# Delta-rule attention with two MLPs: weights converted and split during the attention, half of the second MLP's kept on chip, fillers in another bank, and a searched order

## The chip, the core and the metric

The kernel runs on one core of a Trainium2 chip. Its time is device microseconds (us) of one execution. TensorE (PE) multiplies into PSUM; VectorE (DVE), ScalarE (ACT) and GpSimd (POOL) do the rest; SyncE's queue (SP) issues nearly all transfers between the on-chip memory and DRAM.

## What is computed

Three stages follow one another. `_attn_ref` goes through 768 positions of 32 heads one by one; `_moe_ref` and `_moe2_ref` are two-layer MLPs on 3072 tokens of width 384, with 2048 hidden units and two different activations.

```
for t in range(S):
    kt, vt, bt = (k_n[:, :, t], v[:, :, t], beta[:, :, t, None])
    y[:, :, t] = np.einsum('bhd,bhde->bhe', q[:, :, t], state)
    v_old = np.einsum('bhde,bhd->bhe', state, kt)
    state = state + bt[:, :, :, None] * np.einsum('bhd,bhe->bhde', kt, vt - v_old)
...
P = a[0] + a[1] * h + a[2] * h2 + a[3] * h3
Q = 1.0 + np.abs(b[0]) * np.abs(h) + np.abs(b[1]) * h2
g = P / (Q + 1e-06)
...
sp = np.where(h > 20.0, h, np.log1p(np.exp(np.minimum(h, 20.0))))
g = h * np.tanh(sp)
```

The four weight matrices arrive as 64-bit floats. The kernel turns them into 32-bit ones with integer operations on their two words, and splits every 32-bit operand of an MLP into a high part and the remainder, so that three matmuls replace one.

## The kernel before

**Attention** (line numbers are those of the profile). The 768 positions are 12 chunks of 64, called u. `prepare` (L264) loads and normalizes k and q of a chunk, transposes them (L317) and forms their products (L332), which DVE masks into `gm` and `lg` (L341). `inverse` (L384) takes two chunks together: DVE transposes `lg` (L402), then DVE or POOL runs 30 dependent pairs of small operations (L414, L420) between two scalings by beta (L405, L424), and DVE transposes the result into `xt` (L427). `ON_DVE = (1, 7)` puts the inverses of chunks 0, 1 and 6, 7 on DVE, the other four on POOL. There is one `lg`. `step` (L444) is the recurrence: each chunk needs the state `su` of the one before and its own `xt`: PE (L474, L491, L506, L514, L529), DVE (L482) and ACT (L498, L522, L538) in turn, for two halves of the heads.

**Order.** `Plan` collects these operations with an estimated duration, what they read and write, and a due time (`early`), and lists them by the longest path that remains (`order`, L90). Every engine then runs its part in that order. Where the plan leaves PE idle, `run` (L128) puts in fillers: matmuls of a zero tile (`heat`, L1010) into 128 columns of the PSUM tile `side`. The other 384 columns of `side` hold the DVE's intermediate words of the weight conversion.

**Weights.** `Weights.convert` (L609) handles one of the two matrices of one f (f counts 16 slices of 128 hidden units): a load into `w64` (L616), `mag` on ACT (L628), four DVE operations (L633, L637, L643, L649) into `wm`. During the attention all 32 matrices of the first MLP are converted; those of f = 0 are split into their slot (L659 on ACT, L664 on POOL), the other 30 go unsplit to DRAM (L657). `fetch`, `hi` and `lo` (L684 to L695) bring an f back, copy its high part on ACT (L689) and subtract on POOL or DVE (L693).

**MLPs.** A unit is one group of 512 tokens (six groups) with one f, so 96 units an MLP. A unit has nine matmuls up (L784), elementwise work, and four units later its matmuls down: nine of 512 columns (L870) in the first MLP, twelve of 384 (L903) in the second. `MLP_OPS` lists, for four kinds of unit, in which order the operations of a unit and of older ones are issued; kinds 0, 2 and 3 contain the split `wa`, `wb`, `wB`. The first MLP splits f = 1 to 15 in its first 15 units, from two `wraw` buffers. The second's matrices are converted by `Conv`: 16 of 32 spread over the first MLP, the rest in the first units of the second, four thirds of a matrix a unit; each goes to DRAM, comes back and is split.

## Time and profile before

| | us |
|---|---|
| median of 3 runs (1221.35 to 1222.2) | 1221.74 |
| the profiled execution | 1227.12 |
| its span, from the first to the last instruction | 1225.4 |
| attention, to the start of the first MLP's first matmul | 341.1 |
| first MLP, its first 17 units up | 97.0 |
| first MLP, from there to the second's first matmul | 337.9 |
| second MLP, first 16 units | 101.6 |
| second MLP, the rest | 347.8 |

The stages were cut where PE's matmuls change lines (L784 begins at 341.1, L903's unit 96 at 775.97); the first MLP's units begin one after another, so 341.1 and 438.1 are the starts of units 0 and 17, and 877.56 that of unit 112. The profiled execution is 5.4 us over the median. Engines are busy for 1074.0 us (PE), 756.6 (DVE), 604.9 (ACT) and 520.8 (POOL) of the span, which says little, since the stages differ: PE works without gaps in the last, and in the others something else decides.

### The profile page before, as it was taken

How to read it: one execution, taken by the hardware profiler on the slowest of the kernel's cores; microseconds unless marked ns; L12 is line 12 of the kernel's file. 1: busy time of each engine (PE TensorE's matmuls, PEld its weight loads, DVE VectorE, ACT ScalarE, POOL GpSimd, SP SyncE). 2: the span in 40 equal slices, each digit the busy share in tenths (PEclk: the TensorE clock that was granted, in tenths of full speed). 3: DMA queues.
4: the chain of work that ended last, by engine and by line, in shares of the span. 5: the costliest groups of instructions: out<-in, count | busy, mean ns of one | idle time of the engine just before them, and what ended most of it. 6: DMA issues, size and time to landing. Idle time of an engine off the chain costs nothing.

```text
span 1225.4 us, 24811 instructions
## 1 busy us (share of the span) xinstructions
PE 1074.0 (88%) x10210; PEld 924.5 (75%) x10210; DVE 756.6 (62%) x1226; ACT 604.9 (49%) x1063; POOL 520.8 (42%) x582
## 2 busy tenths in 40 slices
PE   6658876687759899999999999967899999999998
PEld 5557765687746578777787778766799999999997
DVE  5876689775448989989898999876412121212111
ACT  4325533342246788788888888732332333232222
POOL 3184757446036667667676777863300000000000
PEclk9959899697669999999999999988899999999999
DMA  6326743365332310212111121255200000000000
GB/s 119 80 60 155 171 120 87 93 171 137 111 91 68 106 59 28 69 46 65 46 48 63 40 72 28 91 191 167 84 27 26 26 27 26 26 26 1 21 7 26
DMA packets 128322, 89.01 MB, mean 73 GB/s; under 512 B 80592, under 2 KB 113232, under 8 KB 128208
## 3 DMA queue, kind: packets, MB, share of 16 engines
q1 hardware_dynamic: 127952, 87.32, 26.3%
q8 instruction: 80, 1.31, 0.5%
q14 instruction: 34, 0.28, 0.1%
q0 software_dynamic: 256, 0.10, 0.1%
HBM read 61.05 MB, written 26.35 MB: 71 GB/s over the span
## 4 chain that ended last, share of the span: by engine, by line
PE 41%; POOL 13%; DVE 12%; ACT 10%; issue 7%; DMA 5%; SPq 0%; POOLq 0%; DVEq 0%; ACTq 0%
PE h L784 17%; PE o L903 14%; POOL q L827 7%; ACT r L834 3%; POOL r L817 3%; POOL gh L799 2%; ACT q L814 2%; PE c_ps L491 2%; DMA w<-in_moe_w_in_dram 2%; ACT r L836 2%; PE y_ps L529 2%; PE o L870 2%; DMA w<-in_moe_w_out_dram 1%; DVE wm L649 1%; PE c_ps L506 1%
## 5 line engine op out<-in xcount | busy, mean ns | idle before, releaser
L784 PE MATMUL h<-x,w 128*128 128x512 f32 x1728 | 448.3, 404 | 54.9 <-ACT g L894 22.9
L784 PEld LDWEIGHTS h<-x,w 128*128 128x128 f32 x1728 | 327.4, 193 | 139.3 <-ACT g L894 25.2
L799 DVE TENSOR_TENSOR gh<-g,gh 128x512 fp32r<-128x512 f32 x82 | 57.0, 695 | 278.4 <-ACT g L894 278.4
L903 PE MATMUL o<-w,gh 128*128 128x384 f32 x1152 | 218.6, 338 | 0.0
L870 PE MATMUL o<-gh,w 128*128 128x512 f32 x864 | 214.2, 392 | 0.4 <-ACT ev L992 0.4
L903 PEld LDWEIGHTS o<-w,gh 128*128 128x128 f32 x1152 | 206.8, 190 | 8.4
L870 PEld LDWEIGHTS o<-gh,w 128*128 128x128 f32 x864 | 163.2, 189 | 36.5 <-ACT ev L992 2.1
L889 ACT ACTIVATE gh<-h 128x512 fp32r<-128x512 f32 x96 | 57.5, 599 | 218.0 <-PE h L784 217.9
L827 POOL TENSOR_TENSOR q<-q,r 128x512 f32<-128x512 f32 x96 | 127.2, 1325 | 64.7 <-ACT r L821 59.6
L799 POOL TENSOR_TENSOR gh<-g,gh 128x512 fp32r<-128x512 f32 x110 | 150.8, 1371 | 3.0 <-ACT gh L795 3.0
L817 POOL TENSOR_SCALAR r<-q,ab 128x512 f32<-128x512 f32 x61 | 48.8, 800 | 113.3 <-ACT q L814 113.3
L834 ACT ACTIVATE r<-q,cst 128x512 f32<-128x512 f32 x96 | 66.4, 691 | 55.3 <-POOL q L827 55.3
L850 DVE SCALAR_TENSOR_TENSOR q<-q,r 128x512 f32<-128x512 f32 x96 | 65.6, 683 | 25.6 <-ACT r L836 25.4
L841 DVE TENSOR_TENSOR s<-s,h 128x512 f32<-128x512 f32 x96 | 65.4, 681 | 17.1 <-ACT s L823 17.0
L823 ACT ACTIVATE s<-h,ab 128x512 f32<-128x512 f32 x96 | 74.2, 773 | 0.0
L843 DVE SCALAR_TENSOR_TENSOR s<-s,ab,h 128x512 f32<-128x512 f32 x96 | 71.8, 748 | 3.4
L491 PE MATMUL c_ps<-r,xt 32*32 32x48 f32 x1536 | 48.8, 225 | 26.9 <-DVE r L482 22.0
L814 ACT ACTIVATE q<-h 128x512 f32<-128x512 f32 x96 | 57.3, 597 | 30.3 <-PE h L784 26.2
L854 DVE SCALAR_TENSOR_TENSOR r<-s,ab,r 128x512 f32<-128x512 f32 x96 | 71.9, 749 | 0.0
L1012 PE MATMUL side<-ident,zero 128*128 128x128 f32 x194 | 32.4, 323 | 41.0 <-DVE wm L649 17.1
L859 DVE SCALAR_TENSOR_TENSOR g<-q,r 128x512 f32<-128x512 f32 x96 | 65.9, 687 | 3.3
L491 PEld LDWEIGHTS c_ps<-r,xt 32*32 32x32 f32 x1536 | 43.0, 123 | 31.9 <-DVE r L482 22.7
(116 smaller groups left out, 1403.9 us busy)
## 6 DMA issues: line engine op xcount, KB each, us to landing
w<-in_moe_w_in_dram SPq DMA_DIRECT2D x32, 384.0 KB, 3.7
w<-in_moe_w_out_dram SPq DMA_DIRECT2D x32, 384.0 KB, 3.6
w<-wm SPq DMA_DIRECT2D x62, 192.0 KB, 3.6
wraw<-w SPq DMA_DIRECT2D x31, 384.0 KB, 3.1
xraw<-x SPq DMA_DIRECT2D x36, 256.0 KB, 2.8
kn<-in_k_dram SPq DMA_DIRECT2D x48, 96.0 KB, 3.5
qn<-in_q_dram SPq DMA_DIRECT2D x48, 96.0 KB, 3.6
v<-in_v_dram SPq DMA_DIRECT2D x48, 96.0 KB, 3.4
```

Source lines behind the costliest of these rows:

```text
L491: nc.tensor.matmul(out=out(h, rows, n), lhsT=xt[rows, u % 2 * M + W * h + n, :], rhs=r2[rows, W * h + n, :], start=True, stop=True,)
L784: self.nc.tensor.matmul(out=self.st[i]["h"], lhsT=self.w.t[f][:, a, 0, k], rhs=self.x[g][:, b, k], start=(n == 0), stop=(n == 8),)
L799: (nc.gpsimd if engine == "P" else nc.vector).tensor_tensor(out=s["gh"][:, 1], in0=s["g"], in1=s["gh"][:, 0].bitcast(F32), op=ALU.subtract)
L814: nc.scalar.activation(out=s["q"], in_=s["h"], func=ACTF.Abs)
L817: nc.gpsimd.tensor_scalar(out=s["r"], in0=s["q"], scalar1=k["b1"], scalar2=k["b0"], op0=ALU.mult, op1=ALU.add)
L823: nc.scalar.activation(out=s["s"], in_=s["h"], func=ACTF.Identity, scale=k["a3"], bias=k["a2"])
L827: nc.gpsimd.tensor_tensor(out=s["q"], in0=s["q"], in1=s["r"], op=ALU.mult)
L834: nc.scalar.activation(out=s["r"], in_=s["q"], func=ACTF.Ln, bias=k["c"])
L843: nc.vector.scalar_tensor_tensor(out=s["s"], in0=s["s"], scalar=k["a1"], in1=s["h"], op0=ALU.add, op1=ALU.mult)
L854: nc.vector.scalar_tensor_tensor(out=s["r"], in0=s["s"], scalar=k["a0"], in1=s["r"], op0=ALU.add, op1=ALU.mult)
L870: self.nc.tensor.matmul(out=self.acc[g][d], lhsT=self.w.t[f][:, a, 1, d], rhs=self.st[i]["gh"][:, b], start=(first and n == 0), stop=(last ...
L903: self.nc.tensor.matmul(out=self.acc[g][t][:, 0:384], lhsT=self.st[i]["gh"][:, a, t * 128:(t + 1) * 128], rhs=self.w.t[f][:, b, 1].rearran ...
```

## The change

Line numbers of the changed kernel are given with the orders below.

- The first MLP's matrices are split during the attention: f = 2 to 15 first, each into one of two slots (ACT copies the high part, POOL subtracts), from where both parts go to DRAM in one transfer of 768 KB; f = 0 and 1 come last and stay in the slots. The first MLP fetches f = 2 to 15 already split, straight to their slots; its units have no split left.
- Of the second MLP's matrices those of f = 0 to 7 go through DRAM as before; those of f = 8 to 15 are split straight into their slots. In that stage the conversion's words lie in PSUM (a tile of the ring `r`), and `w64`, `wm` and `wraw` have three buffers.
- `side` is gone: fillers write `y_ps`, the words have a tile `word` of their own, and fillers end where `xt0` is first written. There are 62 of them, 194 before.
- A second `lg` shares memory with the first group's `xraw`, which is now one tile; `xs` alternates by pair of chunks. The DVE's second inverse is that of chunks 8, 9.
- The order: `Plan.best` draws 800 changes of the operations' priorities by kind and keeps what makes the planned end no later. Conversions get a due time of `4000 * i - 60000` in place of `3000 * f`.
- Pools of the MLPs wait for the tiles whose memory they take, not for whole pools.

```diff
-FQ = 1
+FQ = 2
+LOOK = 5
+DIRECT = 8
+LATE = 4000
+AHEAD = 60000
...
+    def best(self):
+        def end(order):
+            return max(e for _, e, _ in order)
...
+        for _ in range(self.TRIALS):
+            trial = dict(bias)
+            for k in rng.sample(kinds, rng.choice((1, 2, 4))):
+                trial[k] = trial.get(k, 0) + rng.gauss(0, rng.choice((1000, 5000, 20000)))
+            other = self.order(trial)
+            if end(other) <= end(order):
+                bias, order = trial, other
+        return order
...
+            over = over or until in self.names[i]
             if engine == "PE":
-                if last is not None:
+                if last is not None and not over:
...
-        self.lg, = ring("lg", 1, [128, 2, M, HC])
+        self.lg = ring("lg", 1, [128, 2, M, HC])
+        self.lg.append(spare.rearrange("p k t -> p (k t)")[:, 0:2 * M * HC].rearrange("p (u m t) -> p u m t", u=2, m=M))
...
-        self.heat, self.word = side[:, 0:128], side[:, 128:TOK]
+        self.word, = ring("word", 1, [128, 384], ps)
...
-        j = int(engine == "POOL")
+        j = u // 2 % 2
...
-    ON_DVE = (1, 7)
+    ON_DVE = (1, 9)
...
+        for i, f in enumerate(fs):
+            slot, late = f"w{i % slots}", LATE * i - AHEAD
+            for side in range(2):
...
+                p.add("ACT", 500, out, [m], [slot], early=late)
+                p.add("POOL", 1000, rest, [m], [slot], early=late)
+            if f not in self.kept:
+                p.add("SP", 2500, lambda f=f: self.store(f), [slot], (), more=2500, early=late)
+
+    def store(self, f):
+        self.nc.sync.dma_start(out=self.scratch[f], in_=self.t.pop(f).bitcast(F32))
...
+    def fetch_split(self, f):
+        self.nc.sync.dma_start(out=self.tile(f).bitcast(F32), in_=self.scratch[f])
...
-                self.act.append(side[5])
+                self.act.append(side[5] if j < self.direct else lambda side=side: (side[5](), side[6]()))
...
-                out=at.heat, lhsT=zero, rhs=at.ident, start=False, stop=False, skip_group_check=True
+                out=at.y_ps[:, 0:128], lhsT=zero, rhs=at.ident, start=False, stop=False, skip_group_check=True
...
-        w1.plan(plan, range(NF))
+        w1.plan(plan, [*range(FQ, NF), *range(FQ)])
...
-        plan.run(heat, 200)
-        conv.start()
+        plan.run(heat, 200, "xt0")
...
-        sb.add(sb2, w=16 - FQ, wraw=2, x=1, q=3, s=3, r=2, g=3, gh=5, ev=3)
+        sb.add(sb2, w=16 - FQ, w64=1, wm=1, wraw=3, x=1, q=3, s=3, r=2, g=3, gh=5, ev=3)
...
-        fetch_w = {n: (w1, FQ + 1 + n) for n in range(NF - FQ - 1)}
-        split_w = {n: (w1, FQ + n) for n in range(NF - FQ)}
-        for f in range(NF):
-            fetch_w[n1 - 2 + f] = (w2, f)
+        conv.start()
+        fetch_w = {n: (w1.fetch_split, FQ + LOOK + n) for n in range(NF - FQ - LOOK)}
+        split_w = {}
+        for f in range(DIRECT):
+            fetch_w[n1 - 2 + f] = (w2.fetch, f)
             split_w[n1 - 1 + f] = (w2, f)
...
+                    w2.word = w2.word or ps.tile([128, TOK], F32, "r")[:, 0:384]
```

How the order moves, at three places. On POOL, between the inverse of chunks 2, 3 and that of 4, 5, before (L414, L420 and L424 are the end of an inverse, L405 the beginning of the next, L664 the subtraction for f = 0):

```order
92 L414 TENSOR_TENSOR tmp_153<-xs_148 128x30
93 L420 TENSOR_TENSOR xs_148<-xs_148,tmp_153 128x30
94 L424 TENSOR_TENSOR xs_148<-xs_148,beta_120 128x1024
95 L664 TENSOR_TENSOR w<-wm,w 128x384 x2
96 L360 TENSOR_TENSOR kn_121<-kn_121,nrm_4_164 128x16x48
97 L360 TENSOR_TENSOR kn_122<-kn_122,nrm_4_164 128x16x48
98 L405 TENSOR_TENSOR xs_148<-xs_148,beta_120 128x1024
```

and there in the changed kernel (L442, L448 and L452 end an inverse, L433 begins one, L692 is the subtraction):

```order
95 L448 TENSOR_TENSOR xs_149<-xs_149,tmp_154 128x28x3
96 L692 TENSOR_TENSOR w<-wm,w 128x384
97 L442 TENSOR_TENSOR tmp_154<-xs_149 128x58
98 L448 TENSOR_TENSOR xs_149<-xs_149,tmp_154 128x29x2
99 L442 TENSOR_TENSOR tmp_154<-xs_149 128x30
100 L448 TENSOR_TENSOR xs_149<-xs_149,tmp_154 128x30
101 L452 TENSOR_TENSOR xs_149<-xs_149,beta_121 128x1024
102 L692 TENSOR_TENSOR w<-wm,w 128x384
103 L433 TENSOR_TENSOR xs_148<-xs_148,beta_121 128x1024
```

The next inverse has its own `xs` and `lg` and stands right behind the last; the subtractions stand inside the inverses, 27 of them between the beginning of POOL's first inverse and the end of its last; there are 32 in all, 2 before.

On PE, at the first matmul that needs the last `xt` (chunks 10, 11), before (L1012 is the filler, L491 the matmul by `xt`):

```order
400 L474 MATMUL c_ps_167<-su_142,kq_134 64x48 x16
401 L529 MATMUL y_ps_171<-kq_134,su_142 48x64 x16
402 L1012 MATMUL side_165<-ident_118,zero 128x128 x6
403 L491 MATMUL c_ps_168<-r_145,xt_151 32x48 x16
404 L491 MATMUL c_ps_167<-r_145,xt_151 32x48 x16
```

and there in the changed kernel (L519 is the matmul by `xt`):

```order
393 L557 MATMUL y_ps_172<-gm_140,u_145 48x64 x16
394 L502 MATMUL c_ps_168<-su_143,kq_135 64x48 x16
395 L519 MATMUL c_ps_169<-r_146,xt_152 32x48 x16
396 L557 MATMUL y_ps_172<-kq_135,su_143 48x64 x16
397 L534 MATMUL c_ps_169<-u_145,gm_141 32x48 x16
```

No filler stands between the steps any more.

On SP, at the end of the attention in the changed kernel (L608 stores the attention's last output, L644 loads a matrix of the second MLP, L795 loads the next group's input, L723 fetches split weights):

```order
103 L795 DMA xraw<-x_1_61 128x512 x3
104 L608 DMA x_5_65<-yst_155 48x8x128 x4
105 L644 DMA w_4842<-in_moe_w_in_dram 128x3x128
106 L723 DMA w<-w_2_82 128x1536
107 L723 DMA w<-w_3_83 128x1536
108 L723 DMA w<-w_4_84 128x1536
```

Eleven more rows of L723 follow, down to f = 15; before, L686 fetched unsplit halves of that size at this place, each waiting for one of two buffers.

## Rows read from the trace of the kernel before

**Rows 1.** Windows by stage: busy us of each engine (instructions), then PE clock, DMA share, GB/s.

```profile
0.00:73.80 73.80, 37.95 (x526) 33.75 (x526) 54.27 (x137) 23.02 (x43) 26.01 (x62) 0.88 0.44 82
73.80:306.80 233.00, 184.03 (x5192) 169.22 (x5192) 165.17 (x319) 88.40 (x172) 141.74 (x238) 0.85 0.54 131
306.80:341.10 34.30, 26.83 (x749) 25.39 (x749) 11.81 (x20) 8.66 (x17) 0.00 (x0) 0.73 0.36 105
341.10:438.10 97.00, 75.67 (x271) 54.00 (x271) 76.62 (x102) 62.70 (x101) 55.87 (x47) 0.88 0.26 81
438.10:775.97 337.87, 329.11 (x1423) 266.58 (x1422) 313.15 (x470) 282.17 (x475) 240.13 (x203) 0.99 0.18 53
775.97:877.56 101.59, 77.01 (x325) 63.88 (x325) 72.95 (x91) 36.53 (x61) 57.02 (x35) 0.88 0.50 155
877.56:1225.40 347.84, 343.42 (x1729) 311.66 (x1728) 62.58 (x92) 103.44 (x196) 0.00 (x0) 1.00 0.06 21
```

**Rows 2.** Waits during the attention: who waited for whom, us in total, times, longest.

```profile
POOL xs L405 <- DVE xs L402: 68.0, 3, 27.1
PE side L1012 <- DVE side L637: 11.9, 3, 10.8
```

**Rows 3.** Timeline of POOL: start, us, operation, idle before it and its releaser.

```profile
57.76 2.34 POOL L405 TENSOR_TENSOR xs<-xs,beta 128x1024 f32<-128x1024 f32 x1 [27.14 <-DVE xs L402]
97.42 1.91 POOL L424 TENSOR_TENSOR xs<-xs,beta 128x1024 f32<-128x1024 f32 x1
108.80 1.00 POOL L664 TENSOR_TENSOR w<-wm,w 128x384 fp32r<-128x384 f32 x1 [8.51 <-ACT w L659]
259.19 2.36 POOL L405 TENSOR_TENSOR xs<-xs,beta 128x1024 f32<-128x1024 f32 x1 [25.39 <-DVE xs L402]
```

**Rows 4.** Groups by line, POOL in the attention: count, busy us, mean ns.

```profile
L360 POOL TENSOR_TENSOR kn<-kn,nrm 128x768 f32<-128x768 f32 x10 | 14.7, 1474 | 33.8 <-ACT kq L321 17.1 <-DVE nrm L309 16.7
```

**Rows 5.** Timeline of DVE and PE at the last inverse's end.

```profile
306.75 1.99 DVE L427 STREAM_TRANSPOSE xt<-xs 128x1024 f32<-128x1024 f32 x1
...
312.53 2.93 PE L1012 MATMUL side<-ident,zero 128*128 128x128 f32 x12 [10.83 <-DVE side L637]
```

**Rows 6.** The chain that ended last, there: start, us, what.

```profile
305.81 4.84 DMA w<-in_moe_w_out_dram
310.66 0.02 issue
310.68 0.02 ACTq L628
310.69 0.04 issue
310.74 0.55 ACT wm L628
```

**Rows 7.** Timeline of PE in the first MLP's first units.

```profile
360.61 4.21 PE L784 MATMUL h<-x,w 128*128 128x512 f32 x9 [2.08 <-ACT w L689]
366.89 4.21 PE L784 MATMUL h<-x,w 128*128 128x512 f32 x9 [2.07 <-ACT w L689]
...
385.93 0.98 PE L784 MATMUL h<-x,w 128*128 128x512 f32 x3 [1.27 <-DVE w L693]
```

**Rows 8.** The chain in the second MLP, at its full pace.

```profile
1166.60 2.08 PE h L784 x9
1168.69 2.10 PE o L903 x12
```

**Rows 9.** Timeline of ACT and PE in the second MLP's first units.

```profile
816.69 0.83 ACT L689 CAST w<-wraw 128x768 fp32r<-128x768 f32 x1 [13.72 <-DMA wraw<-w]
...
818.07 4.21 PE L784 MATMUL h<-x,w 128*128 128x512 f32 x9 [9.44 <-ACT g L894]
```

**Rows 10.** The conversion's tiles: durations in ns as min/median/max, first and last start.

```profile
L637 DVE TENSOR_SCALAR side<-side x32: 566/566/567, 76.2 to 324.4; 128x384 int32<-128x384 int32 x32
...
L637 DVE TENSOR_SCALAR wm<-wm x32: 359/361/2024, 419.4 to 864.7; 128x384 int32<-128x384 int32 x32
```

**Rows 11.** DMA issues: KB each, median us to landing; and a window of 2 us, columns as in rows 1.

```profile
wraw<-w SPq DMA_DIRECT2D x31, 384.0 KB, 3.1
...
809.00:811.00 2.00, 0.00 (x0) 0.00 (x0) 0.59 (x3) 0.00 (x0) 0.00 (x0) 1.00 1.01 369
```

**Rows 12.** The page's 40 slices of the span: granted clock in tenths of full speed.

```profile
PEclk9959899697669999999999999988899999999999
```

More of the change, by code (lines that the diff above doesn't have):

```diff
@@ L1 @@
+import random
 from contextlib import ExitStack
@@ L126, in order, with run @@
         return done
-    def run(self, idle, unit):
-        last = None
-        for t, end, i in self.order():
+    TRIALS = 800
+    def best(self):
+        def end(order):
+            return max(e for _, e, _ in order)
+        self.kinds = [(op[0], names[0].strip("0123456789") if names else "") for op, names in zip(self.ops, self.names)]
+        kinds, rng = sorted(set(self.kinds)), random.Random(0)
+        bias, order = {}, self.order()
+        for _ in range(self.TRIALS):
[6 more added lines that the diff above has]
+        return order
+    def run(self, idle, unit, until):
+        last, over = None, False
+        for t, end, i in self.best():
             engine, ns, fn = self.ops[i][:3]
+            over = over or until in self.names[i]
             if engine == "PE":
-                if last is not None:
+                if last is not None and not over:
                     for _ in range(min(6, int((t - last) * 0.6 // unit))):
@@ L373, in prepare @@
                 p.add("DVE", 550, masked(i, d, t, 1), [b], [f"{gmb}{2 * d + i}"])
-                p.add("DVE", 290, masked(i, d, t, 0), [b], [f"lg{u % 2}{2 * d + i}"])
+                p.add("DVE", 290, masked(i, d, t, 0), [b], [f"{lgb}{2 * d + i}"])
         def block(a):
             rows = slice(64 * a + HC, 64 * a + C)
-            return lambda: nc.scalar.copy(out=self.lg[rows, u % 2], in_=gm[rows, :, 0:HC])
+            return lambda: nc.scalar.copy(out=lg[rows, u % 2], in_=gm[rows, :, 0:HC])
         for a in range(2):
-            p.add("ACT", 580, block(a), [f"{gmb}{i}" for i in range(4)], [f"lg{u % 2}{i}" for i in range(4)])
+            p.add("ACT", 580, block(a), [f"{gmb}{i}" for i in range(4)], [f"{lgb}{i}" for i in range(4)])
         if u % 2:
@@ L429, in inverse @@
         whole = 2400 if engine == "POOL" else 1400
-        p.add("DVE", 2000, first, [f"lg{j}{i}" for j in range(2) for i in range(4)], lsb)
+        p.add("DVE", 2000, first, [f"{lgb}{j}{i}" for j in range(2) for i in range(4)], lsb)
         p.add(engine, whole, rows, (), lsb)
@@ L668, in plan @@
     def plan(self, p, fs):
[L670 to L682 removed]
+        slots = len(self.kept)
+        for i, f in enumerate(fs):
+            slot, late = f"w{i % slots}", LATE * i - AHEAD
+            for side in range(2):
+                n = 2 * i + side
+                get, mag, size, sign, low, out, rest = self.convert(f, side)
+                raw, m = f"w64{n % 2}", f"wm{n % 2}"
+                p.add("SP", 1500, get, (), [raw], more=2500, early=late)
+                p.add("ACT", 560, mag, [raw], [m], early=late)
+                p.add("DVE", 1160, size, [m], ["word"], early=late)
+                p.add("DVE", 570, sign, [raw], ["word"], early=late)
+                p.add("DVE", 570, low, [raw, "word"], [m], early=late)
+                p.add("ACT", 500, out, [m], [slot], early=late)
[4 more added lines that the diff above has]
+        self.nc.sync.dma_start(out=self.scratch[f], in_=self.t.pop(f).bitcast(F32))
     def fetch(self, f):
@@ L964, in run @@
             fn()
-    conv = Conv([w2.convert(f, side) for f in range(NF) for side in range(2)])
+    conv = Conv([w2.convert(f, side) for f in range(NF) for side in range(2)], 2 * DIRECT)
     m1 = Mlp1(nc, w1, sb, ps, x1, consts)
@@ L999, in tile_delta_attention_two_mlps @@
     with ExitStack() as actx:
-        at = Attention(actx, tc, q, k, v, beta, x1)
+        m1.xr[0] = sb.tile([128, 3, TOK], F32, "xraw")
+        at = Attention(actx, tc, q, k, v, beta, x1, m1.xr[0])
         at.setup()
@@ L1020, in tile_delta_attention_two_mlps @@
         at.plan(plan)
-        w1.plan(plan, range(NF))
+        w1.plan(plan, [*range(FQ, NF), *range(FQ)])
         late = 20000
-        plan.add("SP", 100, lambda: m1.fetch_x(0), [f"x1_0{p}{j}" for p in range(2) for j in range(2)], ["xr"], more=3000, early=late)
+        plan.add("SP", 100, lambda: m1.fetch_x(0), [f"x1_0{p}{j}" for p in range(2) for j in range(2)], ["xr"] + [f"lg1{u}{j}" for u in range(2) for j in range(4)], more=3000, early=late)
         for n in range(3):
```

71 lines of the change are left out of this document (30 added, 41 removed).

## The prediction

> **What bounds the kernel now.** I read the windows by stage first, since one bound does not hold for the whole span. In the last stage [rows 1] PE is busy throughout at full clock, and the chain alternates between nine matmuls up, 2.08 us, and twelve down, 2.10 us [rows 8]: 4.18 us a unit. Nothing in the change touches it. The stage before the second MLP, 338 us for 79 units, is 4.28 us a unit, with PE busy 97% and DVE 93%: nearly full as well. That leaves three stages in which PE waits: the attention (341.1 us), the first MLP's first 17 units (97.0 us, 5.7 us each) and the second's first 16 (101.6 us, 6.35 us each).
>
> The attention has no full engine: from 73.8 us, when the first `xt` is there, to 341.1 us DVE is busy 165.2 + 11.8 = 177 of 267 us, or 66%, POOL less. The waits tell why: POOL stood still before three inverses for 68.0 us in all [rows 2], 27.1 before its first and 25.4 before its last [rows 3], until DVE had transposed `lg`. Since each engine runs a fixed order and there is one `lg`, the next pair of chunks came late. At the end PE stood 10.83 us before fillers, until DVE had written `side` [rows 5], and the chain shows what was behind it: a weight's transfer, then ACT's `mag`, then the conversion [rows 6]. So the conversion, which nobody needed there, held the recurrence through the bank that it shares with the fillers.
>
> In the first MLP's first units PE waits for ACT's high part and DVE's remainder of the weights, 2 us a unit, at half clock (4.21 us for nine matmuls) [rows 7]. In the second's, ACT waited 13.72 us for a fetched weight and PE 9.44 us behind it [rows 9].
>
> **The sum, part by part.** It is made against the profiled execution, 1227.1 us, which lies 5.4 us above the median.
>
> *Attention: removed, the bank shared with the fillers; added, subtractions on POOL; moved, nearly everything.* I bound its end from both sides. From below by POOL. Its first inverse, from 57.76 to 97.42 + 1.91, took 41.6 us, with two normalizations of k of 1.47 us inside [rows 3, 4], so an inverse is 38.6 us. If POOL begins at 57.8 as before and never waits again, it runs four inverses (154.4 us), six normalizations (8.8 us) and 27 subtractions of 1.00 us [rows 3] by 248 us. DVE's transposition adds 2.0 us [rows 5]. From the end of the fillers at 315.46 (312.53 + 2.93) to the end of the attention before took 25.6 us, so it would end at 276 us. From above by DVE at the share of before. In the new order ten conversion operations and two masks more stand ahead of the first `xt`; at 0.56 us each they make some 6 us, so it comes at 80 us, and 171 us of DVE's work remain (177 less 6). To end at 276 DVE would have to be busy 171 of 196 us, 87%; at the 66% of before the end is at 339 us. I take the share halfway between, 76.5%, because two of the reasons for the idle time are removed (one `lg`, the shared bank) and the third, engines that wait for each other in a fixed order, stays: 80 + 171/0.765 = 304 us, **37 us less**, with 65 less and 2 less as ends.
>
> ACT's 30 more casts, at some 0.5 us (0.83 us is twice the size [rows 9]), make 15 us on an engine that was busy 120 us of 341; they cost nothing while it has gaps, and at most their 15 us without. The 14 transfers of 768 KB in place of 30 of 192 KB carry 5 MB more. The 16 DMA engines were busy for 54% of the stage's middle at 131 GB/s [rows 1], so 5 MB are about 21 us more of 225, a share below 70%. But SP is one queue: a store that waits for a subtraction holds the loads of v behind it, and v has one buffer. That is part of why I stay away from POOL's bound. Of the fillers, 132 disappear; the dozen on the path at the end, 2.93 us [rows 5], is counted above.
>
> *First MLP, first units: removed, ACT's copy (0.83 us) and the remainder on DVE of 15 units; moved, the fetch.* Without the split a unit is the unit of the next stage, 4.28 us, and 17 of them are 72.8 us. I add 2.1 us for the first units, in which PE is half idle: 75 us, **22 us less**. The ends: 73 us; and 88 us, if seven sets of nine matmuls run at the half clock (4.21 in place of 2.1 us). The fetches are twice as large. All 14 stand on SP one behind another, with f = 0 and 1 already in place; at the 369 GB/s of the best window [rows 11] one of 0.79 MB takes 2.1 us, half of a unit, so I cost them at nothing.
>
> *First MLP, middle:* the same operations in the same order but for the third buffers; 0, within 3 us.
>
> *Second MLP, first units: removed, for f = 8 to 15, the store, the fetch, ACT's copy and the remainder; added, a cast and a subtraction of each matrix.* At full pace 16 units are 66.9 us, so 34.7 us are lost now. The matrices that keep the old path are those that were converted long before, and three of them now fit into `wraw`. A matrix is converted in three quarters of a unit, so an f in 1.5 units from unit 97 on, the last around unit 109, and f = 15 is needed at unit 111; I see no wait of that size there. I leave a quarter of the loss for the eight units that still fetch and split: 75.6 us, **26 us less**; ends 35 and 15 less. As to the words in PSUM: on `wm` in SBUF the conversion's second operation took 0.361 us in the median and up to 2.02 us, on `side` in PSUM 0.566 us always [rows 10]. If DVE decides, 32 operations of this kind (two a matrix) are 6.6 us more by the medians and up to 46 us less by the worst; both are beside the path, and I take 0. The Trainium skill (VectorE: DVE Perf Modes, Why PSUM operands drop a tier) speaks against this move: PSUM offers DVE one read port, so a 32-bit operation there loses the mode that streams one tensor through two ports. By that rule alone the sum would be 6.6 us later; the medians agree with it, the maxima say that it is not the whole price.
>
> Sum: 37 + 22 + 26 = 85 us less, 1142 us for a profiled execution, **1137 us** as a median.
>
> **Rivals.**
>
> *1. The attention gains nothing.* Each subtraction waits for a cast, that for DVE, that for a transfer. Of the two subtractions of before one waited 8.51 us [rows 3] and the other not at all. In POOL's bound of 276 us, 27 waits of 2.4 us each bring the end back to 341. Against it: the plan spreads conversions over the whole stage with up to an inverse's length of lead. Then 1137 + 37 = 1174 us.
>
> *2. The first MLP waits for its fetches.* A transfer of 384 KB landed after 3.1 us [rows 11]. If large ones do not overlap, 14 of 6.2 us are 87 us for units 2 to 15, and the stage takes some 92 us instead of 75: 1154 us. Against it: the best window, and five or more are under way at once.
>
> *3. Slower: without fillers PE stays at 1.2 GHz.* In the attention PE's granted clock fell behind each long wait, to 0.5 to 0.7 of full speed in five of the page's first twelve slices [rows 12], and the fillers that stood there are gone. PE's work after 73.8 us is, in full-clock terms, at most 184.0 x 0.85 + 26.8 x 0.73 = 176 us [rows 1]. With a mean clock c the attention then ends at 80 + 176/c. The other stages give 48 us, so the kernel is slower from 341 + 48 = 389 us on, that is below c = 0.57. At 0.5, all of it at 1.2 GHz, the end is 432 us, 91 us later: 1222 + 91 - 48 = 1265 us. Against it: the same work in 224 us, from 80 to 304, keeps PE busy for more than three quarters, and before the clock was 0.85 with fewer matmuls per us. The Trainium skill (TensorE: Matmul & The Clock Gate, HAM oscillation) describes this course: matmuls in short bursts between waits begin each burst at half clock, and so lose much of their speed. By that rule this rival is the result; the slices at 0.6 agree with it, those at 0.9 between short waits do not.
>
> *4. It does nothing that can be told:* gains and losses cancel, 1222 us.
>
> **How the numbers follow.** My forecast (all three stages gain, the attention between 276 and 325 us) has 0.70, with 1107 to 1163 us; rival 1 has 0.14, rival 2 0.09, rival 3 0.05, rival 4 0.02. The range from 1105 to 1175 us holds the forecast with most of its bounds (attention 30 us better; or 20 worse, with 18 us on the two others), rival 2 and about half of rival 1, and leaves out the rest, about 0.2. Within 0.2% (2.4 us), which is about what a measurement can tell from no change, are rival 4's 0.02; slower is rival 3's 0.05; faster 0.93.
>
> **What would show it.** In the windows by stage: the first MLP's first matmul at about 304 us, with DVE above three quarters busy behind 80 us; unit 17 some 75 us later; the second MLP's first 16 units in about 76 us; the last stage unchanged at 4.18 us a unit. Among the waits: no PE wait for a word tile, and POOL's waits for L430 far below 68 us. POOL's waits for ACT's cast of a weight (L692) tell rival 1: 27 us in all would do no harm, 65 would. PE waits for transfers of w in units 2 to 15 would show rival 2, a granted clock around 0.6 in the steps rival 3. I am wrong if the attention ends later than 325 us, or if the stages behind it keep their lengths.

## The result and the profile after

The changed kernel takes **1169.3 us** (median of 4 runs, 1165.57 to 1176.74), the kernel before 1221.55 beside it (4 runs, 1214.55 to 1222.2): a ratio of 0.959, 95% interval 0.953 to 0.965. The forecast was 1137 us, the range 1105 to 1175. Sign and range hold; 32 of the 85 us forecast did not come.

The windows by stage of the profile after (execution 1168.82 us, span 1167.1), with the columns of [rows 1]; the stages are cut at the same places, the attention also at the first `xt` and at the last:

```profile
0.00:83.80 83.80, 43.85 (x588) 38.48 (x588) 58.80 (x148) 27.37 (x51) 35.18 (x72) 0.88 0.47 96
83.80:303.50 219.70, 179.58 (x4986) 164.26 (x4986) 160.86 (x310) 97.73 (x193) 157.19 (x255) 0.79 0.58 157
303.50:329.60 26.10, 23.74 (x823) 22.12 (x823) 8.12 (x16) 8.50 (x17) 4.07 (x4) 0.93 0.40 103
329.60:406.20 76.60, 67.95 (x273) 53.65 (x272) 59.78 (x87) 56.98 (x94) 46.53 (x40) 0.91 0.46 175
406.20:745.30 339.10, 330.42 (x1424) 267.54 (x1422) 312.88 (x469) 282.26 (x475) 240.16 (x203) 0.99 0.17 54
745.30:819.20 73.90, 68.82 (x325) 58.38 (x325) 57.02 (x97) 37.38 (x69) 48.02 (x37) 1.00 0.37 118
819.20:1167.00 347.80, 343.44 (x1730) 311.68 (x1728) 62.56 (x92) 103.45 (x196) 0.63 (x1) 1.00 0.06 21
```

| stage | before | forecast | after |
|---|---|---|---|
| attention | 341.1 | 304 | 329.6 |
| first MLP, 17 units | 97.0 | 75 | 76.6 |
| first MLP, middle | 337.9 | 337.9 | 339.1 |
| second MLP, 16 units | 101.6 | 75.6 | 73.9 |
| second MLP, rest | 347.8 | 347.8 | 347.9 |

The two MLP terms came as sized, 48 us in all. The attention ended at 329.6 us, later than the 325 named as the point at which the prediction is wrong there.

Even its 11.5 us are mostly not the change's. The profiled execution of the kernel before, 1227.12 us, was longer than all 34 timed executions of it (1211.2 to 1226.8 us), and the attention varies from one execution to the next: three kernels below that have the very attention of the changed one ended it at 324.5, 325.6 and 327.7 us. So I give, beside each profile's number, the attention of the median run: the profile's, plus the median time less the profiled execution's. For the kernel before that is 341.1 + 1221.55 - 1227.12 = 335.5 us (with its medians beside the three sets of runs below, 1217.0, 1215.3 and 1219.6, it is 331.0, 329.3 and 333.6), for the changed one 330.1. This puts the whole difference between two executions on the attention, which is an assumption: where the code is the same, the last three stages differ by at most 2 us between profiles, but the first MLP's first units by 5 (73.1 to 78.3). The column is good to some 5 us. **By it the attention gained about 0 to 5 us.**

Who waited in it: the waits of GpSimd from 0 to 330 us in the profile after (us in total, times, longest), against [rows 2]:

```profile
POOL w L692 <- ACT w L687: 36.0, 19, 6.1
POOL kn L387 <- DVE nrm L336: 33.3, 2, 20.8
POOL xs L433 <- DVE xs L430: 22.1, 2, 15.1
```

The waits for `lg` (L430, L402 before) fell from 68.0 to 22.1 us, as the second `lg` should make them. New are 36.0 us before subtractions, between the 27 called harmless and the 65 that would bring rival 1. By this view alone one would put the lost gain on those waits; the runs below show how far that goes.

The first MLP has its longest wait at its start; the timeline of PE:

```profile
329.58 4.37 PE L820 MATMUL h<-x,w 128*128 128x512 f32 x18
338.31 6.58 PE L820 MATMUL h<-x,w 128*128 128x512 f32 x18 [4.35 <-DVE g L895]
```

The waits for the weights' split, 2 us a unit [rows 7], are gone, and no wait for a transfer of `w` took their place (rival 2): units 4 to 13 take 4.1 to 4.3 us each. Units 14 and 15 stay long, 7.4 and 7.0 us.

### The profile page after: what moved, and what is told of

Read it like the earlier page. It is cut to its first block, busy times and chain, and to the rows that moved or that the text cites. A ratio compares the mean times of both kernels' runs of the same rounds, so it can differ in the third digit from the quotient of the medians.

```text
span 1167.1 us, 24624 instructions
## 1 busy us (share of the span) xinstructions
PE 1057.8 (91%) x10140; PEld 916.1 (78%) x10140; DVE 720.0 (62%) x1216; ACT 613.7 (53%) x1093; POOL 531.8 (46%) x607
## 4 chain that ended last, share of the span: by engine, by line
PE 49%; POOL 15%; ACT 12%; DVE 11%; issue 8%; SPq 3%; DMA 2%; POOLq 0%; DVEq 0%; ACTq 0%
PE h L820 18%; PE o L939 17%; POOL q L863 8%; ACT r L870 3%; PE c_ps L519 3%; POOL r L853 3%; ACT q L850 2%; PE y_ps L557 2%; SPq L236 2%; POOL gh L835 2%; ACT r L872 2%; DVE tmp L442 2%; PE o L906 1%; PE t_ps L344 1%; PE c_ps L534 1%
## 5 line engine op out<-in xcount | busy, mean ns | idle before, releaser
L820 PE MATMUL h<-x,w 128*128 128x512 f32 x1728 | 436.6, 397 | 19.9 <-DVE s L879 12.5
L820 PEld LDWEIGHTS h<-x,w 128*128 128x128 f32 x1728 | 324.5, 190 | 94.2 <-DVE s L879 20.1
L835 DVE TENSOR_TENSOR gh<-g,gh 128x512 fp32r<-128x512 f32 x88 | 64.1, 728 | 283.9 <-ACT g L930 283.8
L939 PEld LDWEIGHTS o<-w,gh 128*128 128x128 f32 x1152 | 204.5, 188 | 10.8 <-ACT ev L1028 2.7
L835 POOL TENSOR_TENSOR gh<-g,gh 128x512 fp32r<-128x512 f32 x104 | 136.8, 1315 | 8.9 <-ACT g L930 4.9
L692 POOL TENSOR_TENSOR w<-wm,w 128x384 fp32r<-128x384 f32 x48 | 48.9, 1021 | 52.8 <-ACT w L687 52.7
L448 POOL TENSOR_TENSOR xs<-xs,tmp 128x30 f32<-128x30 f32 (+14 forms) x120 | 62.8, 523 | 9.4
L519 PE MATMUL c_ps<-r,xt 32*32 32x48 f32 x1536 | 49.4, 224 | 18.6 <-DVE xt L455 9.6
L853 POOL TENSOR_SCALAR r<-q,ab 128x512 f32<-128x512 f32 x54 | 43.1, 799 | 43.8 <-ACT q L850 43.8
```

Of the source, the lines that this page charges most:

```text
L519: nc.tensor.matmul(out=out(h, rows, n), lhsT=xt[rows, u % 2 * M + W * h + n, :], rhs=r2[rows, W * h + n, :], start=True, stop=True,)
L820: self.nc.tensor.matmul(out=self.st[i]["h"], lhsT=self.w.t[f][:, a, 0, k], rhs=self.x[g][:, b, k], start=(n == 0), stop=(n == 8),)
L835: (nc.gpsimd if engine == "P" else nc.vector).tensor_tensor(out=s["gh"][:, 1], in0=s["g"], in1=s["gh"][:, 0].bitcast(F32), op=ALU.subtract)
L853: nc.gpsimd.tensor_scalar(out=s["r"], in0=s["q"], scalar1=k["b1"], scalar2=k["b0"], op0=ALU.mult, op1=ALU.add)
L939: self.nc.tensor.matmul(out=self.acc[g][t][:, 0:384], lhsT=self.st[i]["gh"][:, a, t * 128:(t + 1) * 128], rhs=self.w.t[f][:, b, 1].rearran ...
```

## Experiments

Twelve kernels in three sets of four, each set on one chip with runs of the kernel before between them. The last columns are the attention in the profile and in the median run.

| kernel | median us | ratio to before (95%) | attention, profile | median run |
|---|---|---|---|---|
| own_bank | 1217.7 | 1.000 (0.997 to 1.002) | 330.6 | 330.5 |
| no_rest | 1167.1 | 0.957 (0.953 to 0.960) | 331.8 | 330.8 |
| no_conv | 1152.5 | 0.945 (0.941 to 0.950) | 313.0 | 316.4 |
| fillers | 1168.2 | 0.957 (0.953 to 0.962) | 330.5 | 331.0 |
| no_y | 1164.5 | 0.957 (0.951 to 0.963) | 327.0 | 326.0 |
| split_back | 1157.0 | 0.952 (0.947 to 0.956) | 312.1 | 313.0 |
| direct16 | 1175.6 | 0.968 (0.962 to 0.974) | 325.6 | 332.0 |
| words_sbuf | 1179.7 | 0.971 (0.964 to 0.979) | 324.5 | 330.3 |
| no_rest_new_order | 1160.6 | 0.952 (0.947 to 0.956) | 314.0 | 319.4 |
| pe_slow | 1168.4 | 0.958 (0.954 to 0.963) | 332.3 | 331.8 |
| best | 1154.0 | 0.947 (0.943 to 0.951) | 312.6 | 311.9 |
| direct16_sbuf | 1188.1 | 0.975 (0.971 to 0.980) | 327.7 | 328.4 |

### The shared bank alone: own_bank

Made from the kernel before, with the argument `until` of the changed `run`:

```diff
-        side, = ring("side", 1, [128, TOK], ps)
-        self.heat, self.word = side[:, 0:128], side[:, 128:TOK]
+        self.word, = ring("word", 1, [128, 384], ps)
...
-                out=at.heat, lhsT=zero, ...
+                out=at.y_ps[:, 0:128], lhsT=zero, ...
...
-        plan.run(heat, 200)
+        plan.run(heat, 200, "xt0")
```

> The kernel before with one part of the change alone: the fillers go to the bank of y_ps and stop when the first xt is planned, the word tile has a bank of its own; order, splitting and placement of the inverses stay. Theory A (the 11.5 us that the attention gained are the stall of PE behind the shared bank, 16 us at 296.8 to 312.5): the stall is gone, the first MLP begins at 325 to 331 us instead of 341.1, the whole takes 1205 to 1212 us. Rival B (the stall turns into another wait, and the gain came from the new order): the first MLP begins at 338 to 344 us, the whole within 3 us of 1222.

Its profile shows an attention of 330.6 us, which looks like theory A; its time does not: 1217.7 against 1217.0, a ratio of 1.000. (It lies outside both theories' bounds, which were set from 1222 us.) The profiled execution of the kernel before was simply a long one. The stall behind the bank [rows 5] is gone. The waits from 63 to 300 us, first here, then in the kernel before (L407, L404, L493 and L484 are there L405, L402, L491 and L482):

```profile
POOL xs L407 <- DVE xs L404: 42.2, 2, 23.4
PE c_ps L493 <- DVE r L484: 37.3, 7, 21.8
```

```profile
POOL xs L405 <- DVE xs L402: 40.9, 2, 25.4
PE c_ps L491 <- DVE r L482: 22.0, 5, 20.2
PE side L1012 <- DVE wm L649: 17.1, 1, 17.1
```

The longest wait of PE, 21.8 us, is the one for the first `xt` and was there before (20.2). But where fillers waited 17.1 us, up to 224.1 us, the recurrence's matmul now waits 13.6, up to 224.2 us: a wait of the fillers had covered one of the recurrence. What took the place of the last stall, 10.8 us, these profiles do not show. So rival B by the times: the stall was real, but was worth nothing that these runs can tell, which is to 3 us.

### Subtractions left out, in the same order and in an order of their own: no_rest, no_rest_new_order

Made from the changed kernel (both also reuse the two slots of `w`, so that what is stored has been written; the second plans 0 for what is missing):

```diff
-                p.add("POOL", 1000, rest, [m], [slot], early=late)
+                p.add("POOL", 1000, rest if i < 2 else lambda: None, [m], [slot], early=late)
...
+                p.add("POOL", 1000 if i < 2 else 0, rest if i < 2 else lambda: None, [m], [slot], early=late)
```

> The changed kernel in the same planned order, without 28 of the 32 subtractions on GpSimd in the attention (the low parts of 14 of the 16 matrices of the first Mlp are left out; casts, stores and fetches stay). Theory A (the subtractions, 28.3 us of work and 27.6 us of waits for casts between 63 and 301 us, hold the inverses on GpSimd and with them the end, rival 1 of the prediction): the last inverse on GpSimd ends at 245 to 270 us instead of 300.9, the first MLP begins before 308 us, the whole takes 1148 us or less. Rival B (DVE's own inverse and the recurrence set the end, GpSimd only follows): the first MLP begins at 321 us or later, the whole takes 1160 us or more.

The attention of the median run is 330.8 against 330.1 us: no gain. The waits of GpSimd in it, 0 to 330 us:

```profile
POOL kn L387 <- DVE nrm L336: 54.0, 5, 20.2
POOL xs L433 <- DVE xs L430: 38.6, 4, 16.2
POOL w L692 <- ACT w L687: 6.1, 4, 3.7
```

Before casts GpSimd waits 29.9 us less, before DVE 20.7 + 16.5 = 37.2 us more. In this order the wait named in the profile was not the one that held the stage: others, as long, took its place. Theory A seemed dead. But an order that was made around the subtractions cannot use their absence, so they were left out of the plan too:

> As no_rest (28 of the 32 subtractions on GpSimd left out, and with them the low parts of 14 matrices of the first Mlp), but the plan counts the missing ones as nothing and searches an order anew. In the order made for them their absence gave nothing (1167 us), while the kernel that undoes the split, with an order of its own, ended the attention at 312.1 us. Theory A (the 28 us of GpSimd's time are what the split costs, and only the order decides whether their absence can be used): the attention ends at 310 to 318 us, the whole takes 1148 to 1157 us. Rival B (the casts, the two slots and the large stores cost it): the attention ends at 322 us or later, the whole is 1160 us or more.

314.0 us in the profile and 319.4 in the median run, 10.7 less than 330.1; the median time, 1160.6, lies above theory A's bound and on rival B's. So theory A holds in the main and not in full: the 28 us of GpSimd's time cost about 11 us of the attention, once the order may follow. A new order alone does not give that: pe_slow, below, has one too, with all subtractions, and its attention is 331.8.

### The split undone: split_back

```diff
-                p.add("ACT", 500, out, [m], [slot], early=late)
-                p.add("POOL", 1000, rest, [m], [slot], early=late)
-            if f not in self.kept:
-                p.add("SP", 2500, lambda f=f: self.store(f), [slot], (), more=2500, early=late)
+                if f not in self.kept:
+                    p.add("SP", 500, out, [m], (), more=3000, early=late)
+                    continue
+                p.add("ACT", 500, out, [m], [slot], early=late)
+                p.add("POOL", 1000, rest, [m], [slot], early=late)
...
+        fetch_w = {n: (w1.fetch, FQ + 1 + n) for n in range(NF - FQ - 1)}
+        split_w = {n: (w1, FQ + n) for n in range(NF - FQ)}
```

> The changed kernel with the split of the first MLP's weights undone: in the attention the converted matrices of 14 of 16 f go to DRAM as they are (192 KB a side, no cast and no subtraction), and the first MLP fetches and splits one in each of its first 14 units, as before. New banks, two lg, placement of inverses and the searched order stay. Theory A (the attention does not feel the split at all, as leaving out the subtractions suggests, and the first units gain from its absence alone): the attention ends within 5 us of 329.6, the first 17 units take 90 to 97 us instead of 76.6, the whole 1183 to 1190 us. Rival B (the split's casts and large stores do lengthen the attention): the attention ends at 320 us or before, and the whole is 1178 us or less.

Rival B, by more than it asked for: the attention ends at 312.1 us (313.0), **17 us before** the changed kernel's. And the first MLP hardly misses the split: its first 17 units take 81.0 us, though each of units 0 to 13 splits a matrix again as before the change. In ten profiles of kernels whose first MLP fetches its matrices split they took 73.1 to 78.3 us, 75.5 in the mean. The window of the stage here:

```profile
312.10:393.10 81.00, 70.70 (x274) 54.08 (x271) 71.80 (x101) 62.24 (x102) 52.94 (x46) 0.89 0.31 97
```

ACT and DVE do the split inside units of 4.2 to 4.9 us (units 2 to 13). Of the 20.4 us that this stage gained, some 16 are due to what split_back keeps (two matrices instead of one in place, so that unit n splits for unit n + 2, three buffers in `wraw`, and the pools' waits; these were not taken apart), and 4 to 5 to the missing split. Splitting in the attention thus costs 17 us there and saves 5 behind it: split_back is faster than the changed kernel, 1157.0 against 1169.3. Those two were timed in different sets, and the intervals of their ratios just overlap (0.947 to 0.956, 0.953 to 0.965). The pair that settles it stands in the last set: pe_slow splits in the attention, best does not (its longer search ends the attention within 1 us of split_back's), and they took 1165.5 to 1168.9 and 1153.0 to 1154.7 us.

Where the 17 us lie, the transposition into `xt` tells. The row from `s_all` is the first one and names the time at which it began; the row from `xs` has the five later ones, from the time of the first to that of the last. The changed kernel, split_back, pe_slow:

```profile
L455 DVE STREAM_TRANSPOSE xt<-xs x5: 1974/2055/2096, 117.3 to 301.5; 128x1024 f32<-128x1024 f32 x5
L455 DVE STREAM_TRANSPOSE xt<-s_all x1: 1920/1920/1920, 81.9 to 81.9; 128x1024 f32<-128x1024 f32 x1
```

```profile
L455 DVE STREAM_TRANSPOSE xt<-xs x5: 2046/2054/2091, 110.0 to 286.2; 128x1024 f32<-128x1024 f32 x5
L455 DVE STREAM_TRANSPOSE xt<-s_all x1: 1934/1934/1934, 69.9 to 69.9; 128x1024 f32<-128x1024 f32 x1
```

```profile
L455 DVE STREAM_TRANSPOSE xt<-xs x5: 2010/2064/2111, 109.0 to 302.6; 128x1024 f32<-128x1024 f32 x5
L455 DVE STREAM_TRANSPOSE xt<-s_all x1: 1921/1921/1921, 70.5 to 70.5; 128x1024 f32<-128x1024 f32 x1
```

In split_back 12 of them are there at the first `xt`, before the recurrence can begin. But an early first `xt` is not enough: pe_slow has it as early, and its last comes when the changed kernel's does.

### What else could hold the attention: no_conv, fillers, no_y, pe_slow

```diff
 no_conv
+                get, mag, size, sign, low, out, rest = self.convert(f, side) if i < 2 else [lambda f=f: self.tile(f) if f in self.kept else None] * 7
 fillers
-        plan.run(heat, 200, "xt0")
+        plan.run(heat, 200, "")
 no_y
-            p.add("PE", 1080, y_mm(h, part), need, ["y_ps"])
+            p.add("PE", 1080, lambda: None, need, ["y_ps"])
 pe_slow
-    HOP = 60
+    HOP = 100
-        self.ops.append((engine, ns, fn, sorted(need), more, early))
+        self.ops.append((engine, ns * 1.15 if engine == "PE" else ns, fn, sorted(need), more, early))
```

> The changed kernel in the same planned order, without the conversion of 14 of the 16 matrices of the first Mlp in the attention (loads, magnitudes, four DVE operations, cast and subtraction are left out, the 14 stores and fetches of 768 KB stay). It gives the floor of this order. Theory A (the conversion, put between the steps of inverses and recurrence, is what stretches the stage): DVE has some 70 us less to do, the first MLP begins at 290 us or before, the whole takes 1130 us or less. Rival B (inverses, recurrence and the clock of PE set the stage whatever is put between): the first MLP begins at 312 us or later, the whole takes 1152 us or more.

By its numbers rival B, if barely (313.0 us in the profile, 1152.5), but not in its words, for what is put between does cost something: without the conversion DVE is busy 107 us of the 216 from 84 to 300 us instead of 158, and the attention is 14 us shorter (316.4, median run). Four pieces of the chain in no_conv (start, us, what) show what is then last: PE's matmuls one behind another.

```profile
121.45 1.71 PE y_ps L557 x32
123.16 1.05 PE c_ps L502 x26
124.39 1.61 PE y_ps L557 x58
126.00 1.48 PE c_ps L519 x64
```

In the changed kernel the chain of the same kind goes, from 243 to 276 us, through DVE, where the inverse of chunks 8 and 9, the conversion and the recurrence's remainders follow each other:

```profile
246.77 0.57 DVE word L665
247.79 0.45 DVE xs L448
248.24 0.46 DVE r L510
248.71 0.48 DVE word L671
249.21 0.55 DVE wm L677
251.00 1.08 DVE xs L448
```

That stretch is not the whole: from 84 to 300 us seven lines of PE (L344, L359, L502, L519, L534, L542, L557) make 47% of the chain in the changed kernel and 71% in no_conv. Nor does such a share tell the price: in no_rest it is 70%, and its attention takes as long as the changed kernel's.

> The changed kernel with fillers through the whole attention instead of up to the first xt (they write to y_ps, and so wait where ACT still reads it). Theory A (the low clock of PE, 0.65 from 63 to 120 us and 0.80 to 0.81 up to 301, is what stretches the stage, rival 3 of the prediction): the granted clock is above 0.9, the first MLP begins at 315 us or before, the whole takes 1155 us or less. Rival B (PE waits anyway, the clock costs little): the first MLP begins within 4 us of 329.6 us, the whole is within 4 us of 1169 or, if the fillers wait for ACT's copies of y, later.

> The changed kernel in the same planned order, without the matmuls of y in the attention (the attention's output is left out; the copies and stores of y stay). Between 80 and 330 us PE was busy 204 of 250 us, more than DVE (about 180) or GpSimd, and these matmuls are about 45 us of it; leaving out 62 us of DVE's work gave 16 us, leaving out 28 us of GpSimd's gave nothing. Theory A (PE paces the attention from the first xt on, at the clock it is granted): the first MLP begins at 302 us or before instead of 329.6, the whole takes 1142 us or less. Rival B (no engine paces it; the chain of small waits through all four engines does, and PE's work on y lies beside it): the first MLP begins at 320 us or later, the whole takes 1160 us or more.

Here is the window from 84 to 300 us in the changed kernel, with fillers throughout, and without the matmuls of y (columns as above):

```profile
84.00:300.00 216.00, 176.85 (x4886) 161.68 (x4886) 158.23 (x308) 96.31 (x191) 153.53 (x251) 0.79 0.58 156
```

```profile
84.00:300.00 216.00, 188.80 (x5060) 173.16 (x5062) 159.10 (x310) 96.70 (x192) 155.77 (x253) 0.83 0.59 157
```

```profile
84.00:300.00 216.00, 164.70 (x3760) 148.94 (x3760) 159.23 (x310) 96.03 (x192) 155.37 (x254) 0.65 0.58 158
```

Fillers raised the mean granted clock from 0.79 to 0.83 and the time stayed (331.0 against 330.1): rival B by its numbers. But the clock did not reach theory A's 0.9, and the fillers themselves made PE busy 12 us longer; so this shows that the clock could not be bought back in this way, not what it costs. Leaving out the matmuls of y took only 4 us, and a reason stands in the same line: 1126 matmuls fewer, yet PE is busy only 12 us less, since the clock fell from 0.79 to 0.65. A piece of work taken from PE came back as a slower PE. So this run, whose numbers fall on rival B's side, does not settle whether PE paces the stage at a given clock.

> The changed kernel, complete, with one thing else in its plan: matmuls count 15% longer (the granted clock was 0.65 to 0.81 between 63 and 301 us) and a step from engine to engine 100 ns instead of 60. Theory A (the searched order is made for a PE at full clock, so real steps come late and every engine waits in its fixed order): an order made for the slower PE ends the attention at 310 to 320 us instead of 324.5 to 331.8, the whole takes 1148 to 1160 us. Rival B (the order matters little once the work is given): the attention ends between 324 and 332 us, the whole between 1163 and 1171 us.

331.8 us, as before: rival B. The plan's idea of a faster PE is not the cause.

### The second MLP's two parts: direct16, words_sbuf, direct16_sbuf

```diff
 direct16
-DIRECT = 8
+DIRECT = 16
 words_sbuf
-                    w2.word = w2.word or ps.tile([128, TOK], F32, "r")[:, 0:384]
+                    pass
 direct16_sbuf: both
```

> The changed kernel with all 16 matrices of the second MLP through DRAM, as before the change; the third buffer of wraw and the words in PSUM stay. Theory A (the gain of 27.7 us in the second MLP's first 16 units comes from the eight matrices that go straight to their slots): that stage takes 92 to 102 us instead of 73.9, the whole 1187 to 1197 us. Rival B (the third buffer for fetched weights is what took the waits away): the stage stays below 80 us, the whole below 1175 us.

> The changed kernel with the conversion's words of the second MLP in SBUF again (no tile in PSUM for them during the second MLP). Theory A (the words in PSUM are worth nothing either way, as the prediction took it: 0 within 5 us): the second MLP's first 16 units take 71 to 77 us, the whole 1166 to 1172 us. Rival B (in SBUF those operations are stretched beside GpSimd, which now also subtracts): DVE is late, the stage takes 80 us or more, the whole 1175 us or more. Rival C (the page's rule on PSUM operands decides): the stage is 4 to 7 us shorter than 73.9.

> All 16 matrices of the second MLP through DRAM and the conversion's words in SBUF, as both were before the change; the third buffers stay. Its first 16 units took 73.9 us with neither undone, 81.3 with the matrices alone, 88.7 with the words alone, 101.6 before the change. Theory A (the effects add, the third buffers of w64, wm and wraw are worth the rest): 92 to 99 us, the whole 1183 to 1192 us. Rival B (direct matrices and words need each other, the third buffers are worth nothing): 100 to 104 us. Rival C (the words cost only because GpSimd also subtracts beside them): 79 to 85 us.

The stage (units 0 to 15 of the second MLP) in us; where none of this is touched it took 73.9 to 75.3 in nine profiles:

| | words in PSUM | words in SBUF |
|---|---|---|
| 8 matrices straight to their slots | 73.9 | 88.7 |
| all 16 through DRAM | 81.3 | 93.4 |
| before the change, two buffers | | 101.6 |

From the bottom up: 8.2 us of what the change did there besides, the words in PSUM 12.1, the eight direct matrices 7.4, in sum the 27.7. Taken in the other order, the matrices are worth 4.7 and the words 14.8. The three whole kernels lie 6.3, 10.4 and 18.8 us above the changed one, near the 7.4, 14.8 and 19.5 of the table. The 8.2 us are a remainder; no run has the third buffers (of `wraw`, `w64`, `wm`) alone. With them goes an edit that the list of the change leaves out: `m2.pool` gives GpSimd the subtraction of `gh` in every second unit instead of in all of the first 14, so that in this stage it does 11 of them instead of 17. Neither theory of direct16 held (81.3 lies below A's 92 and just above B's 80); rival B of words_sbuf did, and theory A of direct16_sbuf. The part that I had taken at 0 is the largest. The groups by line of DVE's four operations from 745 to 845 us, count, busy us, mean ns; first words_sbuf, then the changed kernel:

```profile
L661 DVE TENSOR_SCALAR wm<-wm 128x384 f32<-128x384 f32 x16 | 7.7, 482 | 0.2
L665 DVE TENSOR_SCALAR wm<-wm 128x384 int32<-128x384 int32 x16 | 10.4, 648 | 0.6
L671 DVE SCALAR_TENSOR_TENSOR wm<-w,wm 128x384 int32<-128x384 int32 x16 | 17.8, 1114 | 0.4
L677 DVE SCALAR_TENSOR_TENSOR wm<-w,wm 128x384 int32<-128x384 int32 x16 | 10.9, 683 | 0.4
```

```profile
L661 DVE TENSOR_SCALAR r<-wm 128x384 f32<-128x384 f32 x16 | 8.9, 559 | 0.5
L665 DVE TENSOR_SCALAR r<-r 128x384 int32<-128x384 int32 x16 | 9.1, 566 | 0.6
L671 DVE SCALAR_TENSOR_TENSOR r<-w,r 128x384 int32<-128x384 int32 x16 | 8.9, 559 | 0.4
L677 DVE SCALAR_TENSOR_TENSOR wm<-w,r 128x384 int32<-128x384 int32 x16 | 8.8, 551 | 0.4
```

These four operations of a matrix cost 2.93 us of DVE with their words in SBUF and 2.24 us in PSUM. `mag`, which in this stage is DVE's too (L652) and lies in SBUF in both, also took longer, 935 against 556 ns. DVE is busy 71.22 us of the stage instead of 57.02:

```profile
735.50:824.20 88.70, 74.75 (x325) 62.43 (x325) 71.22 (x97) 37.44 (x69) 48.00 (x37) 0.92 0.32 98
```

Without direct matrices the stage waits for transfers again, which is what [rows 9] showed; in direct16_sbuf:

```profile
ACT w L726 <- DMA wraw<-w: 39.7, 8, 14.4
```

### Both gains together: best

split_back with pe_slow's two lines and `TRIALS = 2500`.

> The kernel with the first MLP's split undone (split_back, 1157 us) with the plan of pe_slow (matmuls 15% longer, steps of 100 ns) and 2500 trials of the search instead of 800. Theory A (both gains add, since one is GpSimd's time and the other the order): the attention ends at 298 to 308 us instead of 312.1, the whole takes 1143 to 1153 us. Rival B (312 us is where recurrence and clock hold it, as in no_conv with 313.0): the attention ends within 4 us of 312, the whole within 4 us of 1157.

Rival B: the attention (311.9 against 313.0) and the time, 1154.0 us, lie within its bounds, and the two gains do not add. The interval of the ratio (0.943 to 0.951) lies wholly below that of the changed kernel (0.953 to 0.965), and cannot be told from split_back's. **It beats both kernels**: what makes it faster than the changed one is the undone split (pe_slow, with the same two lines of the plan, took 1168.4).

## Why the prediction was right or wrong

**The attention: -37 forecast, 0 to -5 measured.** The step that failed is "I take the share halfway between, 76.5%, because two of the reasons for the idle time are removed". The work in that step was right (171 us; measured 160.86 + 8.12 = 169.0 from 83.8 us on), so was the first `xt` (80; 83.8). DVE's share was not: 169.0 of 245.8 us, 69%, against 66% before. Of the two reasons, the shared bank was none: removing it alone changed nothing (own_bank), though its stall was gone. The upper end, "at the 66% of before the end is at 339 us", was nearer the result than the forecast. And two bounds were missing: the split's 28 us of GpSimd were entered only in POOL's lower bound, where they moved nothing, though with the order they cost 11 us, the whole split 17; and split_back, best, no_conv and no_rest_new_order, which have quite different work on DVE and GpSimd, all end at 312 to 319 us. No run came near POOL's bound of 276 us.

So what the change put beside the split in the attention (two `lg`, `xs` by pair, the inverse of chunks 8 and 9 on DVE, new due times, the searched order) was worth 16 to 23 us, from 329 to 336 us before to 313 in split_back, and the split gave most or all of it back. Which of those gave it was not tried one by one, and what holds the attention at 312 us stays open: less work on DVE or GpSimd helped by 11 to 14 us, less on PE by 4, with a lower clock beside it.

**First MLP's first units: -22 forecast, -20.4 measured.** The size was right. Of the mechanism, "without the split a unit is the unit of the next stage", a quarter, 4 to 5 us, is shown to be so; the other 16 stay when the split is put back, with units of 4.2 to 4.9 us, and so come from what split_back keeps. That the size fits is in part luck. Rival 2 fell.

**Second MLP's first units: -26 forecast, -27.7 measured.** The size was right, and again its parts were not. I gave the gain to the matrices that skip DRAM and 0 to the words in PSUM; the words gave 12 to 15 us, the matrices 5 to 7, and the rest of that stage's edits 8. The sum came out right by luck. "Both are beside the path, and I take 0" was the wrong step: the price lies between the two ends given there, 6.6 us more and 46 less, and it was on the path. Those ends counted two of the four operations; the one that gained most, L671 with 1114 against 559 ns, was not among them. The Trainium skill's rule against this move (VectorE: DVE Perf Modes, Why PSUM operands drop a tier) would have made it 6.6 us slower; the measurement has the other sign.

**Rivals.** Rival 1's outcome for the attention came true, and its total, 1174 us, was nearer than my forecast; its mechanism, waits of subtractions for casts, was there with 36.0 us but held nothing by itself (no_rest). That the time still lies in the range, 1105 to 1175, is owed to the upper end, which took in about half of rival 1. Rival 3, slower below a mean clock of 0.57, did not come: from 84 to 300 us it was 0.79, and fillers that raised it to 0.83 gave nothing. (Of the fillers fewer went than "132 disappear" says: 62 counts calls, 194 counts matmuls in the trace, two a call. The trace of the changed kernel has 124, all before 62 us; of the 194 before, 84 stood behind 74 us.)

## What to carry to other kernels

Where no engine is full, a wait that the profile names can be worth nothing, as two here were, because another lies behind it: take one away alone and look at the times, not at the trace, before adding its length to a sum. Leaving work out under a fixed order, and leaving it out of the order's plan as well, are two experiments, and here they gave 0 and 11 us. And a split, a cast or a copy moved out of a stage is to be priced in the stage that takes it up: here 17 us there for 5 saved.

## What the runs showed of the hardware

DVE's operations on SBUF can stretch beside GpSimd; those with their words in PSUM did not. Second operation of the conversion (L665) on tile `wm`, then on `r` and `word` in PSUM, min/median/max in ns, from the changed kernel:

```profile
L665 DVE TENSOR_SCALAR word<-word x32: 565/566/567, 35.6 to 307.9; 128x384 int32<-128x384 int32 x32
L665 DVE TENSOR_SCALAR wm<-wm x16: 359/360/827, 388.7 to 715.7; 128x384 int32<-128x384 int32 x16
L665 DVE TENSOR_SCALAR r<-r x16: 565/566/567, 757.4 to 807.4; 128x384 int32<-128x384 int32 x16
```

I sorted them by whether GpSimd was busy for more than half of an operation. In PSUM: 0.565 to 0.567 us, and of the 48 GpSimd was busy beside 44. In SBUF, in words_sbuf's second MLP: 0.36 us where GpSimd was busy beside none or an eighth of it (10) and 1.05 to 1.16 with it (6); the third operation, L671, with two inputs in SBUF, 0.55 us without (6) and 1.33 to 2.18 with it (10). The Trainium skill (SBUF — State Buffer, SBUF: two separate sides) gives a reason: a DVE operation in a mode that uses two ports, or with two inputs in SBUF (this only against a GpSimd operation that reads SBUF), and a GpSimd operation hold one pair of ports in turn. The trace agrees for both kinds. So the rule that speaks against a PSUM operand holds where DVE works alone; beside a busy GpSimd the words in PSUM saved 0.5 to 0.6 us of L665, which without GpSimd costs 0.2 more in PSUM, and 0.8 to 1.6 us of L671, which costs nothing more there.

The other was PE's clock: 23% of the matmuls left out between 84 and 300 us, and the granted clock fell from 0.79 to 0.65; PE was busy 12 us less, and the stage 4 us shorter.
